# Halves of the first weight slices, the last two units bank by bank, and another table of offsets in an RWKV and FFN kernel

## The chip, the cores and the metric

The kernel runs on one core of one Trainium2 chip. What counts is the device time in microseconds of one launch, from the inputs in the chip's memory to the output there. The host only lays the arrays out in another order. The kernel before takes 485.24 us, the median of three runs (484.58 to 485.42). The profile is of one more execution, which took 482.58 us.

Five engines work side by side, each through a queue of its own, strictly in order: TensorE (PE, matrix products; PEld is its loading of weights), VectorE (DVE), ScalarE (ACT), GpSimd (POOL) and SyncE (SP), which here only issues DMAs. An instruction that waits holds up all that stands behind it on its engine.

## The reference

Attention with a decaying state, and then a feed-forward layer on its output, all in float32 (batch 4, 8 heads, 768 steps, head size 48; 3072 tokens, 384 wide, 2048 hidden):

```python
for t in range(S):
    cur = np.einsum('bhd,bhe->bhde', u[None] * kt, vt)
    y[:, :, t] = np.einsum('bhd,bhde->bhe', rt, state + cur)
    state = w[None, :, :, None] * state + np.einsum('bhd,bhe->bhde', kt, vt)
...
h = x @ w_in
relu6 = np.clip(h + 3.0, 0.0, 6.0)
g = h * relu6 / 6.0
return (g @ w_out).astype(np.float32)
```

## The kernel before, in words

**Attention.** The 768 steps are cut into 12 chunks of 64, each for two halves of the batch: 24 half-steps `i` = 0 to 23 (`attention`, L566). The state of a half goes from `i` to `i + 2`. A half-step needs scaled keys `ks` and `KH`, scaled receptances `RP`, masked scores `X`, values `V` and the state `St`. TensorE does it in one bundle of small products, here called a *visit* (`visit`, L505): visit `i` adds keys and values of `i` into the bank U (`keep`), computes the scores of `i + 1` into the bank SC, and the outputs of `i` into the bank Y. Most visits hold 64 small products, each of which the profile shows as two, with two weight loads. There is one U, one SC and one Y, so the next visit waits until VectorE and ScalarE have emptied them: `St` (L593), the masked copy of the scores (L564), and the output's high and low float32r parts in the tile `x` (L602, L603). For every odd half-step six small DMAs then move 16 rows each within `x` (L610).

**Feed-forward.** Tokens come in six groups `g` of 512; the 2048 hidden units in 16 slices `f` of 128. A *unit* is one group and one slice. `ffn1` (L615) multiplies `x` by the slice of `w_in` in nine products (three row blocks, and float32r parts high by high, low by high, high by low) into one of two banks h; ScalarE and VectorE make the activation `g` in high and low parts; `ffn2` two units later multiplies it by the slice of `w_out`, nine products into three output banks o0, o1, o2. All `ffn1` and `ffn2` write a common key `ffn`, so they keep the order of the program among themselves. The order of units is: four half-wide ones of group 0, then group 0 up to slice 5, group 1 whole, the rest of group 0, and groups 2 to 5. A unit of group 2 needs the half-steps 8 to 11.

**Weights.** Each slice's `w_in` and `w_out` arrive as one array of 768 64-bit words per row, in three pieces (L359), into one of two buffers `raw`, and six steps split them into `w_hi` and `w_lo` (L369 to L378, L341): `z`, `cv`, `cv` again, `z` again, `w_hi`, `w_lo`, each over the whole width.

**The order of the work.** Nothing runs in the order of the program text. `Schedule` collects operations with costs, what they read and what they write; `order` (L141) then plays them through, picks for each engine the one with the highest priority among those that can begin, and emits all in the order of the start it gave them. The priority is the rest of the chain behind an operation, plus a lead, plus what the table `SHIFT` gives for the operation's number; `HOME` ties some operations to one engine. Where the plan leaves TensorE idle by over 0.9 us, `warm` (L757) puts whole-width float32 products of the identity into the idle bank h1, so that the engine isn't still:

```python
gap = start - free["pe"] - SLACK
...
if gap > 0.3 and not busy:
...
fills.append((free["pe"] + 0.02, c, gap / c * 0.87 / wide))
```

**The end.** After the last `ffn1` three units are left for `ffn2`. The last one is done bank by bank, its third bank in two halves of 256 tokens, the second half into Y (L746 to L750); what the earlier units had summed for that half is copied aside first (L744). ScalarE and VectorE scale the banks (L669, L666) and SP stores them (L672).

Of the kernel before, what the change touches and what calls it, by code (L numbers as in the profile page):

```python
# [10 lines left out]
F32 = mybir.dt.float32  # L11
# [6 lines left out]
ALU = mybir.AluOpType  # L18
# [37 lines left out]
DIRECT = 1  # L56
XBUF = (0, 1, 1, 0, 1, 0)
# [49 lines left out]
}  # L107
HOME = {
    38: "act", 57: "pool", 65: "pool", 83: "dve", 102: "act", 111: "dve", 116: "act", 130: "pool", 135: "dve", 136:
    "dve", 141: "dve", 159: "act", 165: "pool", 171: "pool", 173: "pool", 196: "act", 201: "dve", 211: "act", 215:  # L110
    "act", 216: "pool", 231: "pool", 253: "pool", 254: "dve", 255: "pool", 275: "act", 284: "pool", 285: "dve", 289:
    "dve", 315: "dve", 329: "act", 345: "pool", 362: "dve", 363: "pool", 373: "act", 378: "dve", 392: "dve", 471:
    "dve", 473: "pool", 474: "dve", 476: "dve", 507: "pool", 511: "dve", 512: "pool", 514: "pool", 554: "pool"
# [161 lines left out]
def fast_path(tc, mp, pp, sb, w_hi, w_lo, b3, wm, badi, hps, ops, rT, kT, rt, kt, vt, wp, wu, wcat, out):  # L275
# [80 lines left out]
    def weights(f):  # L356
        for p in range(PIECES):
            cs = slice(NW // PIECES * p, NW // PIECES * (p + 1))
            S.add({"sp": 2.7 / PIECES}, [], [("raw", f % 2, p)], lambda e, cs=cs: dma(raw[f % 2][:, cs], wcat[f][:, cs]))  # L359
        words = "p (n two) -> p n two"  # L360
        rw, zf, bits = raw[f % 2], z[f % 2], cv[f % 2]
# [4 lines left out]
        hi = w_hi[:, f].rearrange("p a m -> p (a m)")  # L366
        lo = w_lo[:, f].rearrange("p a m -> p (a m)")
        kr, kz, kc = ("raw", f % 2), ("z", f % 2), ("cv", f % 2)
        S.add({"act": 0.82, "dve": 0.48}, [kr + (p,) for p in range(PIECES)], [kz], lambda e: act.mul(out=zf, in_=up_f, mul=2.0 ** -112) if e == "act"  # L369
              else dve.tensor_scalar(out=zf, in0=up_f, scalar1=2.0 ** -112, scalar2=None, op0=ALU.mult), port=True)  # L370

        S.add({"act": 0.82}, [kr + (p,) for p in range(PIECES)], [kc], lambda e: act.mul(out=bits, in_=low, mul=ROUND))
# [155 lines left out]
    def prepare(i):  # L528
# [4 lines left out]
        if i < 4:  # L533

            def weigh(e):
                for h in range(4):
                    act.mul(out=RP[q][:, 1, 2 * h:2 * h + 2], in_=RP[q][:, 0, 2 * h:2 * h + 2], mul=uw[:, h:h + 1])
            S.add({"act": 0.9}, [("RP", q), "uw"], [("RU", q)], weigh, LEAD)
        elif i < EARLY:


# [381 lines left out]
```

## Time and profile before

| | us |
|---|---|
| median of three timed runs | 485.24 (484.58 to 485.42) |
| profiled execution | 482.58 |
| its span, first to last instruction | 480.8 |
| PE busy | 465.9 (97%) |
| PE's weight loads busy | 387.5 (81%) |
| VectorE busy | 298.3 (62%) |
| ScalarE busy | 190.1 (40%) |
| GpSimd busy | 48.7 (10%) |

Busy time is what an engine spent in instructions; a product's end is modelled, so busy products overlap. A row of the chain or of a timeline gives the start in us, the length in us, the engine, the line, and how many instructions are merged (xN). What stands in brackets is the idle time of the engine just before, and what ended it; "issue" is idle time that the profile puts down to nothing. Line numbers are of the kernel before; in the changed one the same code stands some lines further on (L341 is L342, L444 is L461, L761 is L777).

### The profile page before, as it was taken

The page shows a single profiled execution, that of the slowest core. Times are in us where ns is not written, and L with a number is a line of the kernel's source. Part 1 is how long each engine was busy: PE and PEld are TensorE (multiplying, and loading weights), DVE is VectorE, ACT ScalarE, POOL GpSimd, SP SyncE. Part 2 cuts the span into 40 slices and gives each one's busy share as a digit, 9 for nine tenths or more (in the row PEclk, how much of TensorE's full clock was granted, in tenths as well). Part 3 has the DMA queues.
Part 4 walks back from the last instruction along what each step waited for, and adds up shares of the span by engine and source line. Part 5 has one row for each costly group of instructions (what it writes and reads, how often), then busy time and mean ns, then how long its engine had stood idle before and what let it go on. Part 6 is the DMA issues. An engine that isn't in the chain of part 4 may idle for free.

```text
span 480.8 us, 11536 instructions
## 1 busy us (share of the span) xinstructions
PE 465.9 (97%) x4959; PEld 387.5 (81%) x4959; DVE 298.3 (62%) x473; ACT 190.1 (40%) x314; POOL 48.7 (10%) x47
## 2 busy tenths in 40 slices
PE   8888999999999999999999999999999999999993
PEld 6777888888888888888888888888888888888883
DVE  6999998989766667554674443786753433333331
ACT  5545766754343323333333333333333333433331
POOL 3224311013001001000100000110000000000000
PEclk9989999999999999999999999999999999999998
DMA  8978643445135322600132500243400010100002
GB/s 217 258 227 250 193 149 131 133 153 146 56 91 163 94 73 65 197 0 1 45 112 72 172 1 0 75 123 102 139 1 0 22 26 7 65 1 1 1 1 71
DMA packets 27180, 43.69 MB, mean 91 GB/s; under 512 B 4049, under 2 KB 12370, under 8 KB 27122
## 3 DMA queue, kind: packets, MB, share of 16 engines
q1 hardware_dynamic: 27026, 42.78, 30.1%
q8 instruction: 41, 0.67, 0.6%
q14 instruction: 17, 0.14, 0.1%
q10 hardware_dynamic: 96, 0.10, 0.1%
HBM read 35.98 MB, written 4.72 MB: 85 GB/s over the span
## 4 chain that ended last, share of the span: by engine, by line
PE 92%; DVE 3%; DMA 2%; issue 1%; SPq 0%; ACT 0%; DVEq 0%
PE o L271 41%; PE h L264 41%; PE Y L444 5%; PE SC L444 3%; DMA rT<-rT 2%; PE U L444 2%; DVE X L559 0%; DVE X L557 0%; DVE RP L341 0%; SPq L350 0%; DVE X L341 0%; DVE St L593 0%; DVE x L603 0%; DVE z L375 0%; DVE cv L373 0%
## 5 line engine op out<-in xcount | busy, mean ns | idle before, releaser
L271 PE MATMUL o<-g,w_hi 128*128 128x512 f32 (+1 forms) x588 | 194.6, 387 | 0.0
L264 PE MATMUL h<-x,w_hi 128*128 128x512 f32 (+1 forms) x588 | 163.8, 387 | 0.0
L631 DVE SCALAR_TENSOR_TENSOR t<-t,h 128x512 f32<-128x512 f32 (+1 forms) x98 | 66.3, 676 | 115.8 <-ACT t L629 115.7
L629 ACT ACTIVATE t<-h,b 128x512 f32<-128x512 f32 (+1 forms) x98 | 66.5, 679 | 169.0 <-PE h L264 168.8
L271 PEld LDWEIGHTS o<-g,w_hi 128*128 128x128 f32 x588 | 109.9, 188 | 22.7
L264 PEld LDWEIGHTS h<-x,w_hi 128*128 128x128 f32 x588 | 108.9, 189 | 22.0
L271 PE MATMUL o<-g,w_lo 128*128 128x512 f32 (+1 forms) x294 | 113.2, 385 | 1.2 <-issue 1.2
L341 DVE TENSOR_TENSOR g<-t,g 128x512 fp32r<-128x512 f32 (+1 forms) x98 | 69.7, 712 | 41.6 <-ACT g L635 41.1
L635 ACT CAST g<-t 128x512 fp32r<-128x512 f32 (+1 forms) x98 | 59.9, 611 | 67.9 <-DVE t L631 67.8
L264 PE MATMUL h<-x,w_lo 128*128 128x512 f32 (+1 forms) x294 | 81.7, 386 | 0.0
L271 PEld LDWEIGHTS o<-g,w_lo 128*128 128x128 f32 x294 | 55.2, 188 | 12.1 <-issue 1.4
L264 PEld LDWEIGHTS h<-x,w_lo 128*128 128x128 f32 x294 | 54.8, 189 | 11.1
L341 POOL TENSOR_TENSOR RP<-rT,E 112x512 f32<-112x512 f32 x13 | 15.4, 1188 | 222.9 <-PE Y L444 200.6
L444 PE MATMUL SC<-RP,ks 48*64 48x64 f32 (+1 forms) x672 | 25.8, 227 | 0.3 <-issue 0.3
L444 PEld LDWEIGHTS U<-V,KH 64*48 64x48 f32 x704 | 18.0, 121 | 7.6 <-issue 5.3
L444 PE MATMUL Y<-RP,St 48*48 48x64 f32 x672 | 23.3, 218 | 0.8 <-issue 0.8
L444 PEld LDWEIGHTS SC<-RP,ks 48*64 48x64 f32 x672 | 22.8, 138 | 1.1 <-issue 1.1
L444 PE MATMUL Y<-X,V 64*48 64x64 f32 x696 | 23.4, 216 | 0.0
L444 PE MATMUL U<-V,KH 64*48 64x48 f32 x704 | 21.0, 208 | 1.0 <-ACT U L585 0.6
L444 PEld LDWEIGHTS Y<-X,V 64*48 64x48 f32 x696 | 21.1, 120 | 0.0
L444 PEld LDWEIGHTS Y<-RP,St 48*48 48x48 f32 x672 | 20.0, 120 | 1.3 <-issue 0.9
L602 ACT CAST x<-Y 112x512 fp32r<-112x512 f32 (+1 forms) x22 | 12.7, 576 | 14.1 <-PE Y L444 14.1
(108 smaller groups left out, 318.1 us busy)
## 6 DMA issues: line engine op xcount, KB each, us to landing
raw<-wcat SPq DMA_DIRECT2D x48, 256.0 KB, 3.9
rT<-rT SPq DMA_DIRECT2D x24, 224.0 KB, 3.7
kT<-kT SPq DMA_DIRECT2D x24, 224.0 KB, 3.8
V<-vt SPq DMA_DIRECT2D x24, 192.0 KB, 2.8
kt<-kt SPq DMA_DIRECT2D x22, 192.0 KB, 3.9
rt<-rt SPq DMA_DIRECT2D x16, 192.0 KB, 4.5
outT<-cv SPq DMA_DIRECT2D x12, 256.0 KB, 2.1
x<-x SPq DMA_DIRECT2D x63, 32.0 KB, 2.0
```

Of the source, the lines that this page charges most:

```text
L264: nc.tensor.matmul(h, (w_hi, w_lo)[wl][:, f, 0, 128 * j:128 * j + 128], x(j, hl), start=(m == 0 and j == 0), stop=(m == 2 and j == 2))
L271: nc.tensor.matmul(o[m], (w_hi, w_lo)[wl][:, f, 1, 128 * m:128 * m + 128], g(hl), start=(clear and k == 0), stop=(last and k == 2), skip_g ...
L341: emit = lambda e: eng[e].tensor_tensor(out=out, in0=in0, in1=in1, op=op)
L444: nc.tensor.matmul(out, lhsT, rhs, start=start, stop=True, skip_group_check=True)
L602: S.add({"act": 0.38 if direct else 0.49}, [ky], [kx + (0,)], lambda e: act.copy(out=hi, in_=yt), LEAD)
L629: S.add({"act": 0.13 + 0.23 * ns}, [("h", n % 2), "b3"], [kt_], lambda e: act.activation(out=t[:, :T], in_=h[:, :T], func=AF.Relu, bias=b3 ...
L631: last = S.add({"dve": 0.05 + 0.28 * ns}, [("h", n % 2), kt_], [kt_], lambda e: dve.scalar_tensor_tensor(out=t[:, :T], in0=t[:, :T], scala ...
L635: S.add({"act": 0.08 + 0.22 * ns}, [kt_], [kg + (0,)], lambda e: act.copy(out=gt[:, 0, :T], in_=t[:, :T]))
```

## The change

Three things change in the code, and two tables with them.

- Slices 0 to 2 (`HALVES = 3`): `w_in` and `w_out` are two separate halves of 384 words, each loaded in two pieces and split by its own six steps; `ffn1` waits for the first half alone and `ffn2` for the second. Slices 3 to 15 stay whole.
- The last two units of `ffn2` are interleaved: bank 2 of the last but one, then bank 0 of both, bank 1 of both, and the two halves of bank 2 of the last.
- The store of the first half of the last bank is issued by ScalarE (`act.dma_start`).
- The planner's cost of one ScalarE step is 1.3 in place of 0.9, and `SHIFT` and `HOME` are new tables, made for the new numbers of the operations. They decide the order.

```diff
+HALVES = 3
 SHIFT = {
-    0: -2, 1: 5.5, 2: -3.7, 3: -0.7, 4: -0.7, 5: -9.8, 7: 2.2, 8: 1, 9: 1, 10: 2.5, 11: -1.4, 12: 7.8, 13: 9.2, 14:
...
+    0: -1.2, 1: 5.5, 2: -3.7, 4: -2.2, 5: -11.1, 6: 7.7, 7: 0.9, 9: 5, 10: 13.2, 11: -3.7, 12: 27.2, 13: 5.8, 14:
...
     def weights(f):
-        for p in range(PIECES):
-            cs = slice(NW // PIECES * p, NW // PIECES * (p + 1))
-            S.add({"sp": 2.7 / PIECES}, [], [("raw", f % 2, p)], lambda e, cs=cs: dma(raw[f % 2][:, cs], wcat[f][:, cs]))
+        halves = ((0,), (1,)) if f < HALVES else ((0, 1),)
+        for part in halves:
+            c0, n = DM * part[0], DM * len(part)
+            pieces = PIECES if len(part) == 2 else 2
+            raws = []
+            for p in range(pieces):
+                cs = slice(c0 + n // pieces * p, c0 + n // pieces * (p + 1))
...
+                S.add({"sp": 2.7 * n / NW / pieces + 0.02 * (len(part) == 1)}, [], keys,
+                      lambda e, cs=cs: dma(raw[f % 2][:, cs], wcat[f][:, cs]))
+            raws = list(dict.fromkeys(raws))
+            split(f, part, c0, n, raws)
+
+    def split(f, part, c0, n, raws):
+        cs = slice(c0, c0 + n)
...
-        tensor_tensor(0.87, 1.9, [kz, ("wh", f)], [("wl", f)], lo, zf, hi.bitcast(F32), ALU.subtract)
+        tensor_tensor(us(0.87), us(1.9), kz + kh, kl, lo, zf, hi.bitcast(F32), ALU.subtract)
...
-            S.add({"act": 0.9}, [("RP", q), "uw"], [("RU", q)], weigh, LEAD)
+            S.add({"act": 1.3}, [("RP", q), "uw"], [("RU", q)], weigh, LEAD)
...
-        reads = [("wh", f), ("wl", f)]
+        reads = [("wh", f, 0), ("wl", f, 0)]
...
-                S.add({"sp": 0.45 * ns}, [kb], [], lambda e, m=m, o=o: dma(
+                queue = act.dma_start if g == NG - 1 and ns == 1 and not sub else dma
+                S.add({"sp": 0.45 * ns}, [kb], [], lambda e, m=m, o=o, queue=queue: queue(
                     out[128 * m:128 * m + 128, t0:t0 + T], o))
...
-    while pend:
-        u = pend.pop(0)
...
+    while len(pend) > 2:
+        ffn2(*pend.pop(0))
+    before, last = pend
+    ffn2(*before, [2])
+    S.add({"act": 0.3}, ["o2"], [("part", 2)], lambda e: act.mul(out=part[:, 2, 256:], in_=ops[2][:, 256:], mul=1.0 / 6.0))
+    for m in range(2):
+        ffn2(*before, [m])
+        ffn2(*last, [m])
+    for c in range(2):
+        ffn2(*last[:3], c, 1, [2], c)
```

What the tables and the planner make of it is seen in the order of the built programs. A row there is one product, or xN alike in a row; the numbers behind the names tell buffers apart (V_84 and V_85, for instance, are the two buffers of V; x_101 holds the tokens of groups 0, 3 and 5, x_102 those of groups 1, 2 and 4; o_68 to o_70 are the banks o0 to o2).

The first place is on TensorE, at the end of the second part of group 0. Before, visit 9 (the rows with V_85) and visit 10 (V_84) stand between products of group 0 (x_101 and the g tiles), as visits 11 and 12 do further on:

```order
L264 MATMUL h_66<-x_101,w_hi 128x512 x3
L444 MATMUL U<-V_85,KH_110 48x48 x2
...
L444 MATMUL Y<-X_87,V_85 48x64 x2
L271 MATMUL o_68<-g_105,w_hi 128x512
...
L264 MATMUL h_66<-x_101,w_lo 128x512 x3
...
L444 MATMUL U<-V_84,KH_109 48x48 x2
...
L444 MATMUL Y<-X_86,V_84 48x64 x2
L271 MATMUL o_68<-g_106,w_hi 128x512
```

With the change the same visit 9 stands behind the last hidden product of group 0, and visits 10, 11 and 12 follow with fillers (the rows of L777) between them; the last row is the first product of group 2:

```order
L272 MATMUL o_70<-g_106,w_hi 128x512
L461 MATMUL U<-V_85,KH_110 48x48 x2
...
L777 MATMUL h_67<-ident 128x356 x3
L461 MATMUL U<-V_84,KH_109 48x48 x2
...
L777 MATMUL h_67<-ident 128x420 x4
...
L777 MATMUL h_67<-ident 128x388 x4
L265 MATMUL h_66<-x_102,w_hi 128x512 x3
```

The row of three fillers stands behind visit 9 and once more behind visit 10, that of 420 columns behind visit 11, that of 388 behind visit 12. Before, there is one filler in the whole program, 444 columns wide, in the start; with the change there are two of 264 columns at that place, and these 14.

The second place is on VectorE, about the split of slice 0 (raw_114, cv_118 and z_116 are its buffers). Before:

```order
L341 TENSOR_TENSOR RP_88<-rT_76,E 112x512
L373 SCALAR_TENSOR_TENSOR cv_118<-raw_114,cv_118 128x768
L603 TENSOR_TENSOR x_101<-Y,x_101 112x4x128
L375 SCALAR_TENSOR_TENSOR z_116<-z_116,cv_118 128x768
L341 TENSOR_TENSOR X_86<-ks_111,RP_88 112x512
...
L341 TENSOR_TENSOR w_lo<-z_116,w_hi 128x768
```

With the change:

```order
L620 TENSOR_TENSOR x_101<-Y,x_101 112x4x128
L342 TENSOR_TENSOR KH_109<-kt_82,TW 128x384
L392 SCALAR_TENSOR_TENSOR z_116<-z_116,cv_118 128x384
L342 TENSOR_TENSOR X_86<-ks_111,RP_88 112x512
L387 TENSOR_SCALAR z_116<-raw_114 128x384
L342 TENSOR_TENSOR w_lo<-z_116,w_hi 128x384
```

The first half's steps stand further ahead, and the second half's follow behind (the row of L387 is already its first).

The third place is the end, on ScalarE (the first three rows, or four) and on SP (the rows behind the line of dots). Before:

```order
L744 ACTIVATE part<-o_70 128x256
L670 ACTIVATE cv_118<-o_68 128x512
L670 ACTIVATE z_116<-o_70 128x256
...
L672 DMA outT<-cv_118 128x512
L672 DMA outT<-cv_119 128x512
L672 DMA outT<-z_116 128x256
L672 DMA outT<-raw_115 128x256
```

With the change:

```order
L761 ACTIVATE part<-o_70 128x256
L687 ACTIVATE cv_118<-o_68 128x512
L687 ACTIVATE z_116<-o_70 128x256
L690 DMA outT<-z_116 128x256
...
L690 DMA outT<-cv_118 128x512
L690 DMA outT<-cv_119 128x512
L690 DMA outT<-raw_115 128x256
```

One of SP's four last stores has moved to ScalarE, behind the step that makes its data.

## Rows read from the trace of the kernel before

**Rows 1.** Windows: length, busy us (count) of PE, PEld, DVE, ACT, POOL; clock, DMA, GB/s.

```profile
0.00:57.27 57.27, 49.65 (x1206) 42.74 (x1210) 50.97 (x96) 30.13 (x62) 18.52 (x24) 0.97 0.83 236
57.27:473.14 415.87, 415.87 (x3756) 344.62 (x3757) 246.54 (x378) 159.63 (x252) 30.22 (x23) 1.00 0.24 70
473.14:480.80 7.66, 0.34 (x3) 0.14 (x2) 0.79 (x2) 0.38 (x1) 0.00 (x0) 0.79 0.32 111
```

**Rows 2.** Chain that ended last: start us, us, what (from its whole length).

```profile
63.53 2.04 PE h L264 x9
...
147.20 2.26 PE o L271 x9
...
171.92 2.26 PE o L271 x9
...
299.11 2.04 PE o L271 x9
303.08 2.26 PE h L264 x9
...
467.33 5.81 PE o L271 x27
```

**Rows 3.** Timeline of PE: start us, us, instruction; whole-width filler products.

```profile
3.31 1.91 PE L410 MATMUL o<-ident 128*128 128x512 f32 x2
5.02 1.49 PE L410 MATMUL U<-ident 128*128 128x384 f32 x2
...
21.67 1.01 PE L761 MATMUL h<-ident 128*128 128x444 f32 x2
```

**Rows 4.** Timeline of DVE around attention visits 9 and 11.

```profile
147.24 0.75 DVE L564 COPY_PREDICATED X<-mask,SC 128x512 f32<-128x512 uint8 x1 [0.47 <-PE Y L444]
...
148.34 0.68 DVE L603 TENSOR_TENSOR x<-Y,x 112x512 fp32r<-112x512 f32 x1
...
172.83 0.68 DVE L603 TENSOR_TENSOR x<-Y,x 112x512 fp32r<-112x512 f32 x1
```

**Rows 5.** Timeline of the SP queue after visit 11.

```profile
173.54 3.92 SPq L610 DMA_DIRECT2D x<-x  x6
```

**Rows 6.** Page, DMA issues: median us from issue to landing at the end.

```profile
x<-x SPq DMA_DIRECT2D x63, 32.0 KB, 2.0
```

**Rows 7.** Waits of PE from 20 to 60 us: us in total, times, longest.

```profile
PE SC L444 <- issue: 1.9, 2, 1.6
```

**Rows 8.** Windows between the ends of such stops of PE.

```profile
23.89:28.99 5.10, 3.09 (x128) 2.87 (x128) 5.10 (x8) 2.86 (x5) 2.95 (x2) 1.00 0.98 299
28.99:40.25 11.26, 10.48 (x254) 9.88 (x255) 10.65 (x17) 5.45 (x10) 2.49 (x2) 0.85 0.60 184
40.25:44.80 4.55, 3.33 (x129) 3.10 (x129) 4.51 (x9) 2.57 (x4) 1.17 (x1) 1.00 0.99 291
44.80:51.36 6.56, 6.21 (x127) 5.42 (x128) 6.56 (x13) 3.98 (x7) 2.52 (x3) 1.00 0.93 234
```

**Rows 9.** Windows of 2 us about the first FFN products.

```profile
28.00:30.00 2.00, 1.01 (x28) 0.99 (x28) 2.00 (x4) 0.52 (x2) 0.67 (x1) 1.00 0.79 270
30.00:32.00 2.00, 2.00 (x13) 1.78 (x15) 1.94 (x4) 0.91 (x2) 0.00 (x0) 0.59 0.33 82
```

**Rows 10.** Timeline of DVE: low part of slice 5.

```profile
61.73 0.95 DVE L341 TENSOR_TENSOR w_lo<-z,w_hi 128x768 fp32r<-128x768 f32 x1
```

**Rows 11.** Window from the first score step to that low part, columns as in rows 1.

```profile
10.09:61.73 51.64, 45.47 (x1237) 41.21 (x1234) 49.36 (x84) 29.28 (x55) 15.62 (x11) 0.97 0.80 231
```

**Rows 12.** Timeline of the SP queue at the end.

```profile
472.75 1.11 SPq L672 DMA_DIRECT2D outT<-cv  x2
473.95 1.46 SPq L672 DMA_DIRECT2D outT<-z  x1
475.51 0.54 SPq L672 DMA_DIRECT2D outT<-raw  x1
```

**Rows 13.** Timeline of DVE at the end.

```profile
473.59 0.42 DVE L666 SCALAR_TENSOR_TENSOR raw<-Y,part 128x256 f32<-128x256 f32 x1
```

More of the change, by code (lines that the diff above doesn't have):

```diff
@@ L56 @@
 DIRECT = 1
+HALVES = 3
 XBUF = (0, 1, 1, 0, 1, 0)
 SHIFT = {
[46 rows of a table removed]
[46 rows of a table added]
 }
 HOME = {
[L109 to L113, printed above, removed]
+    38: "act", 40: "dve", 57: "pool", 65: "pool", 75: "dve", 105: "dve", 109: "act", 110: "dve", 129: "act", 141:
+    "act", 142: "pool", 146: "act", 150: "act", 151: "pool", 157: "pool", 176: "act", 180: "act", 181: "dve", 187:
+    "dve", 188: "pool", 217: "act", 251: "dve", 266: "act", 272: "pool", 292: "dve", 296: "dve", 305: "dve", 307:
+    "pool", 310: "pool", 335: "dve", 346: "dve", 350: "act", 351: "dve", 365: "dve", 379: "act", 383: "dve", 399:
+    "dve", 492: "pool", 495: "dve", 497: "pool", 533: "pool"
 }
@@ L356, in weights @@
     def weights(f):
-        for p in range(PIECES):
-            cs = slice(NW // PIECES * p, NW // PIECES * (p + 1))
-            S.add({"sp": 2.7 / PIECES}, [], [("raw", f % 2, p)], lambda e, cs=cs: dma(raw[f % 2][:, cs], wcat[f][:, cs]))
+        halves = ((0,), (1,)) if f < HALVES else ((0, 1),)
[5 more added lines that the diff above has]
+                cs = slice(c0 + n // pieces * p, c0 + n // pieces * (p + 1))
+                keys = [("raw", f % 2, h, p) for h in part]
+                if len(part) == 2:
+                    keys = [("raw", f % 2, h, x) for h in part for x in range(3)] if p == 0 else [("raw", f % 2, 0, p), ("raw", f % 2, 1, p)]
+                raws += keys
+                S.add({"sp": 2.7 * n / NW / pieces + 0.02 * (len(part) == 1)}, [], keys,
[4 more added lines that the diff above has]
+        cs = slice(c0, c0 + n)
         words = "p (n two) -> p n two"
-        rw, zf, bits = raw[f % 2], z[f % 2], cv[f % 2]
+        rw, zf, bits = raw[f % 2][:, cs], z[f % 2][:, cs], cv[f % 2][:, cs]
         zi = zf.bitcast(I32)
@@ L365, in weights @@
         up_f = rw.bitcast(F32).rearrange(words, two=2)[:, :, 1]
[L366 to L369, printed above, removed]
+        hi = w_hi[:, f].rearrange("p a m -> p (a m)")[:, cs]
+        lo = w_lo[:, f].rearrange("p a m -> p (a m)")[:, cs]
+        kz, kc, kh, kl = ([(name, x, h) for h in part] for name, x in (("z", f % 2), ("cv", f % 2), ("wh", f), ("wl", f)))
+        us = lambda full, fixed=0.07: fixed + (full - fixed) * n / NW
+        S.add({"act": us(0.82), "dve": us(0.48)}, raws, kz, lambda e: act.mul(out=zf, in_=up_f, mul=2.0 ** -112) if e == "act"
               else dve.tensor_scalar(out=zf, in0=up_f, scalar1=2.0 ** -112, scalar2=None, op0=ALU.mult), port=True)
-        S.add({"act": 0.82}, [kr + (p,) for p in range(PIECES)], [kc], lambda e: act.mul(out=bits, in_=low, mul=ROUND))
-        S.add({"dve": 0.87}, [kc] + [kr + (p,) for p in range(PIECES)], [kc], lambda e: dve.scalar_tensor_tensor(
+        S.add({"act": us(0.82)}, raws, kc, lambda e: act.mul(out=bits, in_=low, mul=ROUND))
+        S.add({"dve": us(0.87)}, kc + raws, kc, lambda e: dve.scalar_tensor_tensor(
             out=bits, in0=up_i, scalar=-2 ** 31, in1=bits, op0=ALU.bitwise_and, op1=ALU.bitwise_or), port=True)
-        S.add({"dve": 0.87}, [kz, kc], [kz], lambda e: dve.scalar_tensor_tensor(
+        S.add({"dve": us(0.87)}, kz + kc, kz, lambda e: dve.scalar_tensor_tensor(
             out=zi, in0=zi, scalar=3, in1=bits, op0=ALU.logical_shift_left, op1=ALU.bitwise_or), port=True)
-        S.add({"act": 0.74, "dve": 0.48}, [kz], [("wh", f)], lambda e: act.copy(out=hi, in_=zf) if e == "act"
+        S.add({"act": us(0.74), "dve": us(0.48)}, kz, kh, lambda e: act.copy(out=hi, in_=zf) if e == "act"
               else dve.tensor_copy(hi, zf), port=True)
-        tensor_tensor(0.87, 1.9, [kz, ("wh", f)], [("wl", f)], lo, zf, hi.bitcast(F32), ALU.subtract)
+        tensor_tensor(us(0.87), us(1.9), kz + kh, kl, lo, zf, hi.bitcast(F32), ALU.subtract)
     def consts():
@@ L656, in emit @@
                     begins and c0 == 0 or sub > 0, ends, ms)
-        S.add({"pe": (2.045 if ns == 2 else 1.24) / 3 * len(ms)}, [("g", n % 3, 0), ("g", n % 3, 1), ("wh", f), ("wl", f)],
+        S.add({"pe": (2.045 if ns == 2 else 1.24) / 3 * len(ms)}, [("g", n % 3, 0), ("g", n % 3, 1), ("wh", f, 1), ("wl", f, 1)],
               [ko[m] for m in ms] + ["ffn"], emit, count=6 * len(ms))
@@ L738, in fast_path @@
             ffn2(*pend.pop(0))
-    while pend:
-        u = pend.pop(0)
-        if pend:
-            ffn2(*u)
-            if len(pend) == 1:
-                S.add({"act": 0.3}, ["o2"], [("part", 2)], lambda e: act.mul(out=part[:, 2, 256:], in_=ops[2][:, 256:], mul=1.0 / 6.0))
-        else:
-            n, g, f, _, _ = u
-            for m in range(2):
-                ffn2(*u, [m])
-            for c in range(2):
-                ffn2(n, g, f, c, 1, [2], c)
+    while len(pend) > 2:
[8 more added lines that the diff above has]
+        ffn2(*last[:3], c, 1, [2], c)
     for i, us in SHIFT.items():
```

90 rows, old and new, of the table SHIFT are left out of this document.

## The prediction

> **What bounds the kernel now.** I first cut the span into three windows [rows 1]. From 57.27 to 473.14 us TensorE is busy in every microsecond at full granted clock, while VectorE is busy 246.54 of 415.87 us. Before that it is busy 49.65 of 57.27 us; after it, the last stores run. So whatever is added to TensorE's queue in the middle is paid in full, and savings can come only from the start and the end.
>
> Next I read the chain that ended last [rows 2]. In the middle it is TensorE alone: nine products of a unit in 2.04 us, and where an attention visit stands between two units, it takes 303.08 - 301.15 = 1.93 us, and the unit after it 2.26. No wait shows on either side. The reader is to see that a visit costs little as long as FFN units stand around it: what the next visit needs is made by other engines in that time.
>
> In the start, PE stops for "issue" [rows 7], that is for nothing the profile names. Between the ends of such stops the counts of products plus weight loads are 256, 509, 258 and 255 [rows 8]: instructions arrive in blocks of about 256. One block took 5.10, 11.26 / 2 = 5.63, 4.55 and 6.56 us, with the DMA engines busy 60 to 99%. All these stretches end in a stop, so instruction supply sets the pace from 23.89 to 51.36 us. VectorE is the other limit there: 49.36 of 51.64 us [rows 11].
>
> **The change part by part.** *Visits 9 to 12.* In the order before, FFN units of group 0 stand between these visits. In the order of the change visits 9, 10, 11 and 12 follow one another behind all hidden products of group 0, and between them stand 3, 3, 4 and 4 filler products. Nothing can be moved there by TensorE itself: it takes its queue in order, and the first unit of group 2 needs the rows of all of visits 8 to 11.
>
> The fillers are 3 x 356 + 3 x 356 + 4 x 420 + 4 x 388 = 5,368 columns. A whole-width f32 product of 512 columns took 5.02 - 3.31 = 1.71 us in the first microseconds [rows 3]. The one of 444 columns at 21.67 us took 1.01 us with its drain, against 1.48 at that early pace. Halving the early pace as an estimate for the full clock (0.855 us for 512 columns) gives 0.74 for 444 columns, and the rest is drain. So the fillers are 5,368 / 512 x 0.855 = 8.96 us. Upper bound: with a drain at each, 5,368 / 444 x 1.01 = 12.2. No end is below 8.9, since the products are in the queue.
>
> Do the visits wait longer than the fillers last? A visit needs the score and output banks of the one before emptied. After visit 9, which ended at 147.20, VectorE finished the last copy at 148.34 + 0.68 = 149.02, 1.82 us later [rows 2, 4]; three fillers of 356 columns last 1.78. So the first two gaps are about 1.9 us. The two gaps of four fillers cover the way from visit 11 to group 2: there the split ended at 173.51, 1.59 us after the visit's end at 171.92, six copies were issued in 3.92 us from 173.54 on, and one takes 2.0 us to land [rows 2, 4 to 6]. That is 1.62 + 3.92 + 2.0 = 7.5 us, less visit 12 within it (1.93): 5.6 of gap, against 8 fillers with 5.4 us. In the kernel before, five stages of nine FFN products lay there and no wait. So gaps of 1.9 + 1.9 + 5.6 = 9.4, that is 0.4 beyond the fillers.
>
> A visit is 64 small products of two passes with as many loads, some 256 instructions, so each is one block. In the run of visits a block is used up in 1.93 + 1.85 = 3.8 us, and the fastest seen is 4.55 [rows 8], which would add 0.8 us twice, the slowest 6.56 about 2.7 twice. These were under a busy DMA; with the light one of the middle (0.24 on the mean [rows 1]) I take 0.6 for both together, bounds 0 and 5.4. [...]
>
> Sum for this place: 9.4 + 0.6 = **+10.0 us**, bounds 9 and 15.
>
> *Halves of slices 0 to 2, and the new places in the start.* A whole split step on VectorE becomes two; the nearest rows are other steps at their own widths. Between the first score step (10.09) and the low part of slice 5 (61.73) [rows 10, 11] VectorE runs 85 instructions before and 93 with the change. Two KH products and one RP product fewer, three ks and one X more (112 or 128 rows wide, moved from or to GpSimd), and halves of about 0.55 in place of steps of 0.95 come out within 1 us of each other. So the low part of slice 5 can come earlier only by the idle 51.64 - 49.36 = 2.3 us, and its unit starts at 63.53, 0.85 after it ended (61.73 + 0.95) [rows 2, 10]: at best the middle starts 0.85 + 2.3 = 3.1 us earlier. The block pace says less: it runs through the whole start, and the number of instructions up to visit 7 grows by 4. Visit 6 now stands ahead of a unit of 512 columns, so its block is wanted some 2 us sooner, and the stop grows. What could be gained is that w_in's half of slice 0 is ready sooner; but at 28.99 PE stood for instructions, not for it. Bounds: -3.1 and +1.5 (one more stop like the longest, 1.6 [rows 7]). I take **-0.6**, near the blocks' end, since PE's stops there are for "issue". DMAs: the six halves issue as 12 loads in place of 9, of smaller size; SP issues three more, and since PE stood for instructions and not for a load at those stops, I cost them at nothing (if that cover is gone, three issues delay what is behind them on SP by about the 0.5 us that the last issue took, each [rows 12]). First filler: 2 x 264 columns in place of 444, +0.14.
>
> *The end.* TensorE's last 27 products of 5.81 us [rows 2] stay, in another order. The store of bank 0 can start 0.68 us (three products of 0.227) sooner. SP's issue of the first half of the last bank took 1.46 us and that of the second began only at 475.51, though its data was ready at 473.59 + 0.42 = 474.01 [rows 12, 13]. With the first half on ScalarE's queue, the second can go at about 474.05: -1.46 at most. The two halves then travel together, so some of it comes back: I take **-1.2**, bounds -1.5 and 0 (ScalarE issuing at SP's slow 1.46 and the transfers then meeting). That ScalarE waits before it issues harms nobody, nothing is behind it. [...]
>
> Sum: 10.0 - 0.6 + 0.14 - 1.2 = **+8.3 us**. The profiled execution took 482.58 us (span 480.8 and 1.8 around it), so it would be 490.9. The timed runs have a median of 485.24, 2.66 above the profiled one; on them the change comes to **493.5 us**.
>
> **The rivals.** *The start pays for it (faster).* If the earlier halves remove all of PE's idle time up to 57.27 us (57.27 - 49.65 = 7.6) and also the low clock (0.85 over 11.26 us, so 1.7 us [rows 8]; 0.59 in it, after PE was busy 1.01 of 2 us [rows 9]), the start gives 9.3, the end 1.5, together 10.8 against 10.1: 484.5. It decides only above 8.5 us of gain in the start. For it: w_in's half of slice 0 and the loads of the first keys are ahead. Against: blocks of 256 and VectorE's 96% hold the start.
>
> *TensorE has room in the middle.* If busy products hid room, gaps and fillers would be absorbed: -0.6 - 1.2 gives 483.4. Weight loads are busy only 344.62 of 415.87 us, 83% [rows 1]. Against: nine products take 2.04 us again and again with no stop, and the fillers are products themselves. [...]
>
> *The run of visits costs more.* Each visit stops for its block at 6.56 us, and PE's clock falls to the lower level as at 30 us: 10.0 becomes 15 to 17, the time 498 to 501. For it: the blocks and the clock of the start [rows 8, 9]. Against: light DMA, and fillers keep PE busy.
>
> *The order does not do what it shows*: visits arrive so late in the kernel before as well that the gaps are hidden in it. Then all is within 1 us of 485. Against: no wait of PE from 57 to 473 us.
>
> **How the numbers follow.** The forecast, +5 to +12, has 0.72. The dearer run of visits has 0.14. A start that gives 3 to 7 us, leaving +1 to +5, has 0.05. The start that pays for it all 0.04, room in the middle 0.02, no change 0.03. Leaving out the last three, and parts of the two ends, the range is 488.5 to 499. Faster or slower means by over 0.2% (1 us, what a measurement of this kernel can tell): faster 0.06, within 0.03, slower 0.91.
>
> **What would show it.** In the profile of the changed kernel the windows should have a place near 170 us where weight loads and FFN products fall off for about 17 us, 14 filler products (28 records) on the filler's line, VectorE's output split as what visits wait for, and PE busy by some 9 us more in total. The two halves' store should be issued within 0.6 us of each other at the end. Stops for "issue" inside visits 10 and 11 would show the block term. I am wrong if the middle shows no such place, or if visit 7 starts before 50 us in place of 57.27.

## The result, and the profile after

The kernel with the change takes 491.89 us, the median of four runs (489.70 to 493.88), against 485.33 for the kernel before in the same rounds: a ratio of 1.0143, with a 95% interval of 1.0110 to 1.0176. In a later comparison on one chip it was 492.69 against 485.31, 1.0152 (1.0119 to 1.0186). The forecast was 493.5. Two executions far off all others, one of 1196 us (of the kernel with visit 9 put back) and one of 527 us (of the new start alone), are left out of the ratios below.

The profiled execution took 493.88 us, its span 492.2. Cut as in [rows 1], now into the start (up to the second FFN unit in a row at the steady pace of 2.04 us), the stretch up to visit 9, the run of visits 9 to 12, the rest, and the end:

```profile
0.00:64.04 64.04, 55.21 (x1342) 48.51 (x1343) 55.36 (x110) 35.28 (x75) 18.83 (x26) 0.95 0.75 219
64.04:178.40 114.36, 114.36 (x628) 94.41 (x630) 86.72 (x127) 53.45 (x81) 4.92 (x4) 1.00 0.35 106
178.40:195.96 17.56, 17.56 (x542) 12.66 (x542) 13.99 (x23) 3.62 (x8) 3.55 (x3) 1.00 0.31 85
195.96:484.99 289.03, 289.03 (x2486) 239.04 (x2484) 144.05 (x229) 97.53 (x157) 12.30 (x10) 1.00 0.18 53
```

TensorE has no idle time in the middle, as before. The third row is new: 17.56 us in which no FFN product stands. The chain of waits there, start, length, what (the visits' own small pieces left out), answers to [rows 2]:

```profile
176.37 2.04 PE o L272 x9
...
180.34 1.99 PE h L777 x6
...
184.27 1.99 PE h L777 x6
...
188.20 3.02 PE h L777 x8
...
193.16 2.80 PE h L777 x8
195.96 2.09 PE h L265 x9
```

The four blocks on the fillers' line make 1.99 + 1.99 + 3.02 + 2.80 = 9.80 us, and the four visits the remaining 7.76. No wait stands on the chain between visits and fillers, and no stop for "issue", which the visits of the start have (2.9 us on the bank U and 2.3 on SC in this trace).

Reading one trace against another needs care here. The nine output products that begin the steady pace start at 64.04 us in this trace and at 61.48 in that of before; but that place moves from one execution to the next (below). What hardly moves is the stretch from there to the end of TensorE's last 27 products. The rows it is read from, before (with the last row of [rows 2]) and after:

```profile
61.48 2.04 PE o L271 x9
```

```profile
64.04 2.04 PE o L272 x9
...
478.84 5.81 PE o L272 x27
```

| kernel (trace) | steady pace from | last product ends | stretch | from there to the span's end |
|---|---|---|---|---|
| before | 61.48 | 473.14 | 411.66 | 7.66 |
| after | 64.04 | 484.65 | 420.61 | 7.55 |
| after, second trace | 62.85 | 483.59 | 420.74 | 7.41 |

The stretch grew by 8.95 and 9.08 us. The end got no shorter to speak of.

### The profile page after: what moved, and what is told of

Read it like the earlier page. It is cut to its first block, busy times and chain, and to the rows that moved or that the text cites. A ratio compares the mean times of both kernels' runs of the same rounds, so it can differ in the third digit from the quotient of the medians.

```text
span 492.2 us, 11613 instructions
## 1 busy us (share of the span) xinstructions
PE 476.2 (97%) x4989; PEld 394.6 (80%) x4989; DVE 300.6 (61%) x489; ACT 189.9 (39%) x320; POOL 39.6 (8%) x43
## 4 chain that ended last, share of the span: by engine, by line
PE 92%; DVE 3%; DMA 1%; issue 1%; ACT 0%; SPq 0%
PE h L265 40%; PE o L272 40%; PE Y L461 5%; PE h L777 2%; PE SC L461 2%; PE U L461 2%; DMA kT<-kT 1%; PE o L461 1%; DVE ks L342 1%; DVE RP L342 1%; DMA wpt<-wp 0%; DVE E L440 0%; DVE z L392 0%; DVE w_lo L342 0%; DVE St L610 0%
## 5 line engine op out<-in xcount | busy, mean ns | idle before, releaser
L342 DVE TENSOR_TENSOR g<-t,g 128x512 fp32r<-128x512 f32 (+1 forms) x98 | 66.6, 680 | 43.1 <-ACT g L652 42.5
```

The lines of the kernel that those rows point to most:

```text
L342: emit = lambda e: eng[e].tensor_tensor(out=out, in0=in0, in1=in1, op=op)
```

## The experiments

All were timed in five rounds against the kernel before on the same chip. "Run" below is a run of visits with no FFN unit between them.

**Visit 9 put back among the units.** The kernel after, one entry less:

```diff
-    ... 535: 0.7, 536: -35, 537: 4.2, ...
+    ... 535: 0.7, 537: 4.2, ...
```

> The kernel after with one entry of the table taken out, that of visit 9's TensorE work (536: -35), so that visits 9 to 12 stand apart again, each between FFN units, as in the kernel before; start and end stay those of the kernel after. Theory (the run of four visits costs 9 us, and start and end together are worth about -1.8 as forecast): 491.9 - 9 = 483, between 482 and 484.5. Rival (the start lost the 2.5 us by which visit 7 came later in the profile of after): 485.3 + 2.4 = 487.7. Rival (TensorE had room in the middle, the loss is elsewhere): 491 to 492.

It took 485.0 us, 0.9992 of before (0.9971 to 1.0013), half a microsecond above the theory's range. The visits stand apart again, as the units of 2.26 us behind them show:

```profile
160.15 2.26 PE o L272 x9
...
166.38 2.26 PE o L272 x9
...
172.62 2.26 PE o L272 x9
```

The stretch is 411.65, that of before to 0.01 us. So the one entry makes the run, and without it the loss is gone. By the medians, though, the run is worth 6.9 us and by the stretch 9.0; that was still open here.

**The same run made in the kernel before.**

```diff
-    ... 515: 3.2, ...
+    ... 515: -35, ...
```

> The kernel before with one entry of its table changed, that of visit 9's TensorE work (515: 3.2 becomes -35): visits 9 to 12 then stand behind one another there too, with 16 fillers in them; start and end stay as they were. Theory: +9 to +10.5, so 494.5 to 496. Rival (the run costs nothing by itself, since TensorE has room): 485 to 486. Rival (the run costs about 4 and the start of the kernel after the rest): 489 to 490.

It took 495.54 us, 1.0212 (1.0180 to 1.0245), +10.4, and the stretch is 422.59, +10.93: here the planner put 15 fillers of 6,260 columns into the run, 892 columns more than in the kernel after (the 16 of the expectation count the one of the start). The rows:

```profile
63.88 2.04 PE o L271 x9
...
480.66 5.81 PE o L271 x27
```

The change's three edits of the code have no part in this loss, and TensorE has no room in the middle. Weight loads were busy 19.87 of the 28.00 us from 174 to 202 us of this trace, products 27.73; no part of the run went into what the loads left.

**A run of two.** The same entry at another value, so that only visit 12 follows a visit directly:

```diff
-    ... 515: 3.2, ...
+    ... 515: -10, ...
```

> The kernel before with its table's entry for visit 9's TensorE work at -10 in place of 3.2: visits 9 and 10 then still stand each by itself between FFN units, and only 11 and 12 follow each other with none between, with 8 fillers, 3 behind visit 11 and 5 behind visit 12. Theory (each visit followed by no FFN unit costs its own wait): the two blocks of fillers of these sizes took 1.99 and 3.82 us in the run of four in before, less 0.22 twice for what the FFN unit behind a lone visit takes longer: +5.4, so 490 to 491. Rival (the whole cost comes with the way from the last visit through the transfers to group 2, however long the run): +10, 495. Rival (a run of two is hidden by FFN units before it): 485 to 486.

It took 489.72 us, 1.0087 (1.0056 to 1.0119). The stretch is 417.12, +5.46, with the two blocks of fillers in their expected sizes:

```profile
185.63 1.99 PE h L761 x6
...
189.56 3.82 PE h L761 x10
193.39 2.10 PE h L264 x9
```

So the price is a sum over the gaps: 5.81 less 0.22 twice makes 5.37 of the 5.46. Neither the length of the run nor the transfers alone set it.

**The run without its fillers.** The kernel after, with the two fillers of the start alone:

```diff
-            warm(*fill.pop(0)[1:])
+            n_fill = fill.pop(0)[1:]
+            if start < DENSE:
+                warm(*n_fill)
```

> The kernel after without the 14 filler products inside visits 9 to 12 (the two of the start stay; no result reads them). Theory (the fillers stand where TensorE would wait for the visit's own chain on VectorE and ScalarE in any case): 1.5 us less at most, 490.5 to 491.9. Rival (the fillers are themselves the cost, and the visits would run on without them): 5 to 9 us less, 483 to 487. Rival (without them the granted clock falls inside the run): 2 to 10 us more, 494 to 502.

It took 492.16 us, 1.0143 (1.0116 to 1.0169): no better, and 0.3 above the theory's range. Its chain of waits shows what the fillers had covered:

```profile
178.83 0.73 DVE X L581
179.56 0.67 DVE x L620
...
182.41 0.73 DVE X L581
183.14 0.65 DVE x L620
...
186.03 0.72 DVE X L581
186.75 0.65 DVE x L620
187.41 0.26 SPq L351
...
190.05 3.12 DMA x<-x
193.17 0.04 issue
193.22 4.40 PE h L265 x9
```

After visits 9 and 10 the chain goes for 1.44 and 1.42 us through the masked scores and the split of the output; from visit 11's end at 186.03 to the first product of group 2 at 193.22 it is 7.19 us, through the split, SP's issues (2.64, two loads and the first three copies) and the fourth copy, which lands 3.12 after its issue; SP issues the last two meanwhile. From the run's start at 176.92 to that product it is 16.30 us, 1.26 less than with fillers. But the clock falls:

```profile
186.00:188.00 2.00, 0.02 (x2) 0.00 (x0) 1.37 (x2) 0.97 (x2) 0.00 (x0) 1.00 0.49 128
...
190.00:192.00 2.00, 1.74 (x84) 1.52 (x74) 1.93 (x4) 0.22 (x1) 0.00 (x0) 0.64 0.30 72
192.00:194.00 2.00, 0.78 (x2) 0.52 (x2) 1.83 (x4) 0.36 (x1) 0.00 (x0) 0.50 0.16 34
194.00:196.00 2.00, 2.00 (x6) 1.41 (x6) 0.00 (x0) 0.00 (x0) 0.00 (x0) 0.50 0.78 246
```

TensorE was busy 0.02 of 2 us from 186 on (visit 12 waited 3.2 us for its load of V), and the granted clock, the third number from the end of a row, goes to 0.64 and 0.50. The first unit takes 4.40 us in place of 2.09, so 2.3 are given back, and the stretch is 421.70, 1.0 longer than with fillers. The fillers are not the cost: they stand in a wait, overfill it by 1.3 us, and save the clock (1.00 with them).

**The new end alone**, in the kernel before (order of the last units, and the store on ScalarE):

```diff
+    for m in range(2):
+        ffn2(*before, [m])
+        ffn2(*last, [m])
...
+                queue = act.dma_start if g == NG - 1 and ns == 1 and not sub else dma
```

> The kernel before with the end of the kernel after alone: the last two units bank by bank, and the third of the last four half stores issued by ScalarE. Theory (the forecast's term): -1.2, 484.1, with the two last stores issued within 0.6 us. Rival (what the profile of after shows: the stores are issued sooner and land 4.3 us after their issue instead): -0.1, 485.2. Rival (the store on ScalarE's queue is dearer): +0.5 or more.

It took 484.63 us, 0.9989 (0.9968 to 1.0010): no difference that can be told, and too wide an interval to tell -1.2 from nothing. The traces tell more. Those of the kernel after answer to [rows 12] (SP's queue, then ScalarE's):

```profile
483.58 1.79 SPq L690 DMA_DIRECT2D outT<-cv  x2
...
485.55 0.33 SPq L690 DMA_DIRECT2D outT<-raw  x1
```

```profile
485.08 0.39 ACTq L690 DMA_DIRECT2D outT<-z  x1
```

The two issues lie 0.47 us apart, and the last comes 0.90 us after TensorE's end, against 475.51 - 473.14 = 2.37 before. The issue is 1.47 sooner than in that trace, as forecast, and 1.06 to 1.43 sooner than in five more with the old end; the span's end is not. From TensorE's end to the span's end it took 7.66, 7.13, 7.00, 7.00, 6.84 and 7.05 us in six traces with the old end (mean 7.11), and 7.55, 7.41, 7.34, 6.62, 7.45 and 7.40 in six with the new one (mean 7.30). The DMA issues of the end, in the trace of the kernel after, with the us from issue to landing last:

```profile
outT<-cv SPq DMA_DIRECT2D x2, 256.0 KB, 2.5
outT<-z ACTq DMA_DIRECT2D x1, 128.0 KB, 2.4
outT<-raw SPq DMA_DIRECT2D x1, 128.0 KB, 4.3
```

The half that goes last takes 1.9 us longer to land than its twin. Two windows of the same trace (the last two numbers are the busy share of the DMA engines and GB/s):

```profile
487.00:488.00 1.00, 0.00 (x0) 0.00 (x0) 0.00 (x0) 0.00 (x0) 0.00 (x0) 1.00 0.53 164
488.00:489.00 1.00, 0.00 (x0) 0.00 (x0) 0.00 (x0) 0.00 (x0) 0.00 (x0) 1.00 0.00 0
```

From 488 to 491 us the DMA engines moved nothing, and the half landed at 489.85: that wait is not for its bytes.

**The new start alone**, with the end of before and without the entry 536:

```diff
-    ... 535: 0.7, 536: -35, 537: 4.2, ...
+    ... 535: 0.7, 537: 4.2, ...
...
-                queue = act.dma_start if g == NG - 1 and ns == 1 and not sub else dma
+                queue = dma
```

> The kernel before with the start of the kernel after alone: the first three slices' halves apart and the offsets of after, without its entry for visit 9 and with the end and the stores of before. Theory (the forecast's term of -0.6, and what the kernel with visit 9 put back showed, 0.9992 of before): 484.5 to 485.2. Rival (the 2.5 us by which visit 7 came later in the profile of after belong to this start): 487 to 488.

It took 482.71 us, 0.9945 (0.9925 to 0.9965), faster than before and below both expectations. Yet up to the last two units this program has the very instructions of the first experiment, which measured 485.0. So the two, and one with the store back on SP, were measured side by side.

**The second measurements.**

> The kernel with visit 9 put back, once more, beside the one that also has the end of before. The two differ in nothing until the last two FFN units, and yet one measured 485.0 and the other 482.7. Theory (the difference is of the chip or the hour, and the start of after is worth about -2 in both): 482.2 to 483.2. Rival (something in the new end makes this kernel's start longer by 2): 484.5 to 485.5 again.

> The kernel with the start of after and the end of before, once more. Theory (the new start brings 2 to 2.6): 482.3 to 483.3, below before by more than the interval. Rival (the first measurement was low by chance): 484.5 to 485.5.

> The kernel with visit 9 put back, with the third of the last four half stores issued by SyncE, as in before, while the last two units keep the order bank by bank. Theory (neither the order of the last units nor the queue of one store reaches the start): the same as the kernel with the store on ScalarE within 0.5, its end longer by 0 to 0.6 for one more issue on SyncE. Rival (the store on ScalarE is what makes that kernel's start longer): 482 to 483 here, and 485 there.

Visit 9 put back: 482.93, 0.9963 (0.9943 to 0.9983). The new start with the old end: 483.22, 0.9969 (0.9950 to 0.9988). The store on SP: 483.66, 0.9972 (0.9946 to 0.9998). The three agree. Why the first measurement gave 485.0 stays open: its interval lies above that of the new start with the old end (0.9971 to 1.0013 against 0.9925 to 0.9965), and it was made on another chip, so it may be chance or the chip. The mean of the five ratios is 0.9968, that is -1.5 us, for the new start with either end. Without the run the new start beats both kernels; with the old end it did so in both measurements. With the store on SP the end was not longer by 0 to 0.6, as the theory had it, but shorter: 6.75 us against 7.40 in the kernel beside it, with the last issue 1.29 us after TensorE's end. That is one trace of each, and the six with the store on ScalarE spread from 6.62 to 7.55.

**The kernel after, a second trace.**

> The kernel after once more, beside the others on one chip, for a second trace. Theory (the run of visits costs 9 us, as the stretch from the first FFN unit at its steady pace to TensorE's end shows: 420.95 us against 411.65 in the kernel with visit 9 put back): the stretch is 421 again, and the time 9 above that kernel's 485.0, 493.5 to 494.5. Rival (it costs 7, as the medians say, 491.9 against 485.0, and the stretch varies from run to run): 491.5 to 492.5, with a stretch of 419 or less in the new trace.

It took 492.69 us, 1.0152 (1.0119 to 1.0186), between the two expectations, and its stretch is 420.74 (the 420.95 of the expectation counts on to 484.99, 0.34 us past the last product's end in the chain). So the run costs 9.0 to 9.1 us in each trace, and what stood open closes nearly: 9.0 for the run less some 1.5 for the start is 7.5, against 6.6 and 7.4 measured.

**More fillers in the start**, in the kernel before, in visit 5 ahead of the products that stopped for "issue":

```diff
+        def busy(n, k):
+            for _ in range(2):
+                nc.tensor.matmul(hps[1][:, :444], ident, ..., start=True, stop=True)
...
-            calls = [(score, k) for k in range(8)] + [(self_weight, k) ...
+            calls = [(score, k) for k in range(8)] + [(busy, 0)] * (i == 4) + [(self_weight, k) ...
```

> The kernel before with four more filler products of 444 columns in visit 5, where TensorE stood from 26.7 to 27.1 and from 27.4 to 29.0 us, ahead of the products that wait there (no result reads them). Theory (the clock's fall to 0.5 between 30 and 34 us follows from that standstill and costs its 1.7 us): the clock stays at 1.0 there and the time is 483.4 to 484.2. Rival (VectorE, busy 15.7 of the 16 us from 20 to 36, and the weights' transfers set the start, not TensorE's clock): the clock stays up and the time is unchanged, 484.8 to 485.4. Rival (the fillers push the visit back): +0.5 to +2.

It took 488.06 us, 1.0059 (1.0039 to 1.0080), against 485.31, slower by 2.8, more than any of the expectations. The clock did stay up where it fell before (0.57 on the mean of the same 4 us). First two windows, then the chain of waits:

```profile
26.00:30.00 4.00, 3.88 (x32) 1.90 (x28) 4.00 (x7) 2.69 (x4) 1.60 (x2) 1.00 0.99 282
30.00:34.00 4.00, 3.60 (x79) 3.23 (x79) 3.28 (x6) 1.28 (x2) 0.00 (x0) 1.00 0.43 115
```

```profile
26.69 2.06 PE h L460 x5
28.87 1.39 PE h L460 x3
30.25 1.05 PE SC L444 x32
```

But the fillers lasted until 30.25, and the products behind them ended at 31.30, against 29.96 before (27 products of 0.97 from 28.99). The visit came 1.3 us later. Nor is that the only difference: the planner counts the new products among the visit's instructions and made another order for the other engines too. On VectorE, for instance, KH now stands ahead of the split of the output (38.62 and 39.08 us), where it stood behind it (39.90 and 37.52). From 54 to 62 us the granted clock is 0.82 and 0.75, where it was 1.00, and TensorE waits for VectorE twice for 1.7 us, which it did not before. So this run tells neither what the clock's fall at 30 us costs nor what the four fillers cost by themselves.

## Why the prediction was right, point by point

- **Visits 9 to 12: the mechanism and most of the size were right.** Forecast +10.0, measured 9.0. The 14 fillers took 9.80 us for the 8.96 estimated, that is 9.80 / 5,368 x 512 = 0.93 for 512 columns where the forecast had 0.855. Its halving of the early pace was an estimate; measured, the 1.71 us of the first microseconds [rows 3] became 0.93, at a granted clock of 1.00 in both places. 0.22 four times comes off, since no single unit behind a lone visit takes 2.26. This subtraction the forecast did not make. Its gaps can be seen one by one in the run without fillers, each shorter than taken: 1.44 and 1.42 for the 1.9 (a path to 1.82, [rows 4]), 7.19 for the 7.5 from visit 11 to group 2. In that path it took 4.99 us from the first copy's issue at 188.23 to the product, in place of 3.92 + 2.0 [rows 5, 6], though two loads stood ahead of the copies. So the gaps did not reach 0.4 beyond the fillers: these overfill them.
- **Instruction blocks, +0.6: nothing.** No stop for "issue" stands in the run: its 1,084 products and loads, 271 in 17.56 / 4 = 4.4 us, fillers included, came without one. In the start of the same trace 774, 253 and 256 lie between the ends of such stops (24.87, 39.21, 43.68 and 50.33 us). Without the fillers visits 9 to 11 ended 3.58 and 3.62 us apart, below the 3.8 of the forecast, and there was no such stop either.
- **Start, -0.6: the sign was right, the size on the small side.** About -1.5 by the five ratios, within the bounds of -3.1 and +1.5. In the profile of after alone it looks like a loss of 2.56 us. In eight traces with the new start the steady pace began at 59.25 to 64.04 us, in four with the old one at 61.48 to 64.98. What in the new start brings the gain (halves, or offsets) was not tried apart.
- **End, -1.2: this step failed.** The issue came 1.47 us sooner and nothing followed from it. The forecast took the last issue for what sets the end. What came of it is that the last landing takes 4.3 us; 485.55 + 4.3 = 489.85, and the span ends 2.35 later. The two halves sharing the DMA engines, by which the forecast took some of the gain back, do not explain it: these moved nothing from 488 to 491 us. What holds that landing, and what the time behind it is, stays open. Of the 1.46 us of SP's issue, the most that the forecast thought could be gained, nothing showed at the span's end (7.30 us behind the last product on the mean, 7.11 with the old end).
- **The rivals.** That the start pays for it all falls with its 1.5 us. Room in the middle falls with the run made in the kernel before. The dearer run would have shown stops and a lower clock in it; the clock is 1.00 there, and falls only without the fillers. That the order doesn't do what it shows falls with the windows.

The terms as measured, +9.0, some -1.5 (with the first fillers) and about +0.2, make +7.7 for the 8.3 forecast: an end that gave nothing and a start that gave more nearly made up for each other, and in the run the block term and the wait beyond the fillers, neither of which came, stood against fillers priced 0.84 too low. So it is in part luck that the forecast landed closer than its terms.

## What to carry to other kernels

Where one engine is busy without a gap, a small piece of work with a long way through other engines costs no more than its own time only as long as other work stands between it and the next such piece (here 1.93 us, and 0.22 on the unit behind it, against 17.56 / 4 = 4.39 in the run); count the gaps that an order leaves between them, and price each by its own path. A single entry of a planner's table can undo that, so look at the order it makes, not at the entry. Where the start moves from one execution to the next (here the steady pace began at 64.04 and 62.85 us in two traces of one kernel), compare stretches that begin behind it.

## What had not been expected of the hardware

- The stretch of 411.66 us came out at 411.64 to 411.68 in five traces of four kernels with different starts and ends, while the place where it began moved by 2.55 us. Three traces of two more kernels gave more: 411.85 and 413.06 with the new start and the old end (a unit of 2.23 us behind that place in the one, in the other a unit that began at 68.97 us, when a copy had landed at 68.92), and 412.54 with the four fillers in visit 5.
- A last store issued 1.47 us sooner after the last product, its twin on a second queue, did not bring the span's end sooner (7.30 us after that product against 7.11, means of six traces each): it landed 4.3 us after its issue, and the DMA engines were idle for the last 1.85 of them.
- With 3.45 us of fillers in what had been a standstill of 0.4 and 1.6 us the granted clock stayed at 1.00 from 30 to 34 us (0.57 before), but fell to 0.82 and 0.75 from 54 to 62 us, where it had been 1.00.
